# Second layer of a mixture of experts as seven block products in passes two and three, on one core

## The chip, the core and the metric

One core of a Trainium2 chip runs the kernel. Its engines work side by side, each through its own queue in order: TensorE (PE, matmuls; PEld is its weight loads), VectorE (DVE), ScalarE (ACT), GpSimd (POOL) and SyncE (SP, which here issues every DMA). The metric is the time of the program on the device in microseconds, the median of several runs.

## The reference

```python
def _moe_ref(x, w_gate, w1, w2):          # x: attention's output, 2304 tokens x 512
    logits = x @ w_gate                   # 8 experts
    logits = logits - logits.max()
    P = np.exp(logits)
    for _ in range(8):                    # Sinkhorn: rows and columns in turn
        P /= P.sum(1, keepdims=True) + 1e-09
        P /= P.sum(0, keepdims=True) + 1e-09
        P *= N / E
    out = np.zeros((N, D), dtype=np.float32)
    for e in range(E):
        h = np.maximum(x @ w1[e], 0.0)    # 512 -> 1024
        ye = h @ w2[e]                    # 1024 -> 512
        out += P[:, e:e + 1] * ye
    return out
```

`x` comes from a sparse attention (4 batches, 8 heads, 576 positions, head size 64; half of the heads see the last 32 positions, half every 32nd).

## The kernel before

A product of two f32 matrices is made of three matmuls: each operand is split into a part `hi` (ScalarE copies it into the matmul's own f32r format) and the rest `lo` (a subtraction), and hi·hi, hi·lo and lo·hi are summed in PSUM.

The program has three stretches. First the attention, and beside it expert 0 (`layer1`, `layer2`, no gate yet). From about 160 us on, one "slot" after the other of expert 0's second half runs; between its matmuls stand the gate's Sinkhorn iterations (`gating`) and `build_s`, which reads a piece of x back from DRAM (`sx<-xd`), adds and subtracts its blocks and stores the results to DRAM (`sd`). Then come experts 1 to 7, in three passes over 768 tokens each. A pass has 28 groups: 7 experts by 4 slices of the hidden layer, 84 groups in all; `step(g)` is written once for each. In it the order of the code is the order on each engine:

- the last two products of group g-1's first layer (t4 and w22: banks `bb`, `bc`), and DVE's sums and rectified parts of them;
- five products of group g's first layer (`ba`, `bb`, `bc`). The first layer is made of seven block products for eight (blocks of 384 tokens, 256 inputs and 128 hidden units): sums of x blocks (`sd`) with sums of W1 blocks, and sums of the results on DVE (L624). A bank is used for two products with a DVE sum between: t3 adds onto the bank `bb` from which `u2` was read.
- the second layer of group g-1 (`second`, L604): six tiles of 128 tokens, each with 2 hidden slices x 3 matmuls of 128x512; then L611 on DVE multiplies by the gate and adds to `acc`, which holds all 18 token tiles in SBUF.

W1's sums are made in the first pass, split, and stored to DRAM (`wd`, 1792 KB a group); the later passes read them back (L554). W2's blocks are read and split again in every pass (L165 on ACT, L166 on POOL). At a pass's end the seven x operands of the next pass are loaded, each behind the last product that uses the old one (`mul`).

```python
mul(g, "w11", "x11", ba, True)
nc.scalar.activation(m1, ba[:, :TN], AF.Copy)
mul(g, "t2", "s2", bb, True)
plus(u2, bb, m1)
...
mul(g, "t3", "s3", bb, False)
```

## Time and profile before

| | us |
|---|---|
| median of 3 runs | 1611.75 (1611.43 to 1613.36) |
| the profiled execution | 1613.57, span of its core 1611.8 |
| PE busy in the span | 1594.4 (99%) |
| DVE, ACT, POOL busy | 932.4, 493.5, 551.0 |
| DMA | 285.30 MB, mean 177 GB/s |
| mean granted TensorE clock | 0.995 of full speed |

The profiled execution took 1613.57 us, of which 1.8 lie outside the span. "PE busy" is no sign that PE works at its peak, because a matmul's own time overlaps its neighbours'; how fast matmuls follow each other is read from the chain of waits, which gives runs of like instructions with their start and length.

### The profile page before, as it was taken

The page shows a single profiled execution, that of the slowest core. Times are in us where ns is not written, and L with a number is a line of the kernel's source. Part 1 is how long each engine was busy: PE and PEld are TensorE (multiplying, and loading weights), DVE is VectorE, ACT ScalarE, POOL GpSimd, SP SyncE. Part 2 cuts the span into 40 slices and gives each one's busy share as a digit, 9 for nine tenths or more (in the row PEclk, how much of TensorE's full clock was granted, in tenths as well). Part 3 has the DMA queues.
Part 4 walks back from the last instruction along what each step waited for, and adds up shares of the span by engine and source line. Part 5 has one row for each costly group of instructions (what it writes and reads, how often), then busy time and mean ns, then how long its engine had stood idle before and what let it go on. Part 6 is the DMA issues. An engine that isn't in the chain of part 4 may idle for free.

```text
span 1611.8 us, 23077 instructions
## 1 busy us (share of the span) xinstructions
PE 1594.4 (99%) x8779; PEld 1426.0 (88%) x8779; DVE 932.4 (58%) x1896; ACT 493.5 (31%) x1186; POOL 551.0 (34%) x482
## 2 busy tenths in 40 slices
PE   7999999999999999999999999999999999999999
PEld 5888888898989989899898998989989899898997
DVE  4665254466566666666556665566655666556665
ACT  6565222333333333342222222223222222222221
POOL 4222333387677766641312222111111111111111
PEclk8999999999999999999999999999999999999999
DMA  6553424564675656559444544544664344443441
GB/s 202 189 166 111 163 92 170 186 225 167 213 248 170 211 191 212 189 211 342 158 164 164 209 148 157 193 144 163 229 253 165 131 164 143 159 168 131 163 143 73
DMA packets 109455, 285.30 MB, mean 177 GB/s; under 512 B 9120, under 2 KB 62880, under 8 KB 98592
## 3 DMA queue, kind: packets, MB, share of 16 engines
q1 hardware_dynamic: 109344, 283.82, 50.7%
q8 instruction: 69, 1.13, 0.3%
q14 instruction: 42, 0.34, 0.1%
HBM read 208.81 MB, written 74.97 MB: 176 GB/s over the span
## 4 chain that ended last, share of the span: by engine, by line
PE 97%; DVE 1%; DMA 1%; ACT 1%; issue 0%; SPq 0%; POOL 0%; ACTq 0%; POOLq 0%; DVEq 0%
PE yg L604 43%; PE bb L589 16%; PE bc L589 11%; PE ba L589 11%; PE y L414 6%; PE ph L390 6%; PE tp L268 1%; PE pv L281 1%; ACT sm L244 1%; PE sc L225 1%; PE pl L324 1%; PE sc L208 0%; PE pv L295 0%; DMA reg<-sd 0%; DMA qk<-in_qkv 0%; DMA v<-in_qkv 0%
## 5 line engine op out<-in xcount | busy, mean ns | idle before, releaser
L604 PE MATMUL yg<-w2g,h 128*128 128x512 f32 x3024 | 702.8, 390 | 0.0
L604 PEld LDWEIGHTS yg<-w2g,h 128*128 128x128 f32 x3024 | 566.3, 188 | 115.2 <-DVE acc L611 0.4
L611 DVE SCALAR_TENSOR_TENSOR acc<-yg,gate,acc 128x512 f32<-128x512 f32 x504 | 378.2, 751 | 237.8 <-PE yg L604 237.6
L166 POOL TENSOR_TENSOR w2g<-r,w2g 128x512 fp32r<-128x512 f32 x168 | 219.6, 1328 | 721.0 <-ACT w2g L165 721.0
L589 PE MATMUL bb<-reg 128*128 128x384 f32 x1512 | 305.0, 336 | 0.5 <-DVE h L397 0.4
L589 PEld LDWEIGHTS bb<-reg 128*128 128x128 f32 x1512 | 268.0, 188 | 7.7 <-DVE h L397 0.7
L628 ACT ACTIVATE h<-m 128x384 fp32r<-128x384 f32 x84 | 44.2, 526 | 553.6 <-DVE m L624 553.6
L589 PE MATMUL ba<-reg 128*128 128x384 f32 x1008 | 201.7, 334 | 0.0
L589 PE MATMUL bc<-reg 128*128 128x384 f32 x1008 | 201.7, 334 | 0.0
L589 PEld LDWEIGHTS bc<-reg 128*128 128x128 f32 x1008 | 177.8, 188 | 0.0
L589 PEld LDWEIGHTS ba<-reg 128*128 128x128 f32 x1008 | 177.2, 188 | 0.1
L628 ACT ACTIVATE h<-u 128x384 fp32r<-128x384 f32 x168 | 88.3, 526 | 194.2 <-DVE u L624 194.2
L632 DVE SCALAR_TENSOR_TENSOR h<-ba,h 128x384 fp32r<-128x384 f32 x84 | 46.8, 558 | 162.9 <-ACT h L628 162.9
L624 DVE TENSOR_TENSOR u<-bc,u 128x384 f32<-128x384 f32 x168 | 93.7, 557 | 43.4 <-PE bc L589 40.5
L624 DVE TENSOR_TENSOR u<-bb,m 128x384 f32<-128x384 f32 x168 | 93.7, 558 | 37.9 <-PE bb L589 29.5
L390 PE MATMUL ph<-reg,w 128*128 128x256 f32 (+1 forms) x672 | 114.5, 320 | 0.0
L414 PE MATMUL y<-w,h 128*128 128x512 f32 x432 | 110.7, 398 | 0.0
L390 PEld LDWEIGHTS ph<-reg,w 128*128 128x128 f32 x672 | 97.0, 192 | 7.8
L632 DVE SCALAR_TENSOR_TENSOR h<-u,h 128x384 fp32r<-128x384 f32 x168 | 97.7, 582 | 10.1
L628 ACT ACTIVATE h<-ba 128x384 fp32r<-128x384 f32 x84 | 41.3, 492 | 187.8 <-PE ba L589 187.8
L165 ACT ACTIVATE w2g<-r 128x512 fp32r<-128x512 f32 x168 | 95.6, 616 | 0.0
L414 PEld LDWEIGHTS y<-w,h 128*128 128x128 f32 x432 | 78.2, 188 | 17.4
(82 smaller groups left out, 1038.8 us busy)
## 6 DMA issues: line engine op xcount, KB each, us to landing
reg<-wd SPq DMA_DIRECT2D x56, 1792.0 KB, 6.7
wd<-reg SPq DMA_DIRECT2D x28, 1792.0 KB, 6.9
r<-in_w SPq DMA_DIRECT2D x168, 256.0 KB, 2.9
...
```

The costliest lines, as they stand in the source:

```text
L165: nc.scalar.activation(hi, src, AF.Copy)
L166: nc.gpsimd.tensor_tensor(lo, src, hi.bitcast(F32), op=ALU.subtract)
L225: nc.tensor.matmul(scs[j][:m, i, :m], t[sl, i * m : (i + 1) * m], t[sl, nq + i * m : nq + (i + 1) * m], start=True, stop=True,)
L244: nc.scalar.activation(sm[:, i, :], sm[:, i, :], AF.Exp, bias=mx[:rows, i : i + 1], scale=-1.0, accum_out=sums[:rows, j * n + i : j * n + ...
L390: nc.tensor.matmul(ph[:, :n], w[:, i, dt, :], xv(x, dt, c0, n), start=(k == 0), stop=(k == 3 * NDT - 1),)
L414: nc.tensor.matmul(y, h[:, a, i * P : (i + 1) * P], w[:, b, :], start=(ft == 0 and first), stop=(ft == FH - 1 and a == 1),)
L589: nc.tensor.matmul(out[:, :TN], w[:, i, k, :], xops[x][:, xi, k, :], start=(start and n == 0), stop=(n == 5), skip_group_check=True,)
L604: nc.tensor.matmul(y, hg[g, i // 3, f][:, a, o : o + P], w2s[g][f][:, b, :], start=(f == 0 and a + b == 0), stop=(f == 1 and a == 1),)
L611: nc.vector.scalar_tensor_tensor(acc[:, t, :], y, gate[:, t, e : e + 1], acc[:, t, :], op0=ALU.mult, op1=ALU.add)
L624: nc.vector.tensor_tensor(o, bank[:, :TN], s, op=ALU.add)
L628: nc.scalar.activation(hg[g, i, f][:, 0], src[:, :TN], AF.Relu)
L632: nc.vector.scalar_tensor_tensor(h[:, 1], src[:, :TN], 0.0, h[:, 0].bitcast(F32), op0=ALU.max, op1=ALU.subtract)
```

## The change

In the second and third pass, 26 of the 28 groups of a pass (all but the last two, `LAST = 2`) make their second layer from seven block products too. The blocks are 384 tokens, 128 hidden units and 256 outputs. In parts:

- The gate multiplies the rectified first layer (`gated`, on DVE), since products of sums can't be scaled afterwards. The gate is turned into rows beside the first pass (`gate_rows`: 14 small transposes on PE) and read back for all partitions, one expert at a time (`load_gate`).
- POOL adds and subtracts the gated blocks (`s1`, `m1`, `r11`, `s4`) and makes the `lo` parts of all seven operands; ACT makes the `hi` parts.
- `second_strassen`: 7 products x 2 halves of the outputs, 3 matmuls of 128x384 each, outputs transposed (weights stand still, tokens stream). DVE adds each of the 14 results to a sum over the groups (`total`); in the first group of a pass ACT copies it.
- At the end of such a pass `combine` makes four blocks from the seven totals (4 additions on DVE, 3 on POOL, 128x768 each), and `turn` transposes them on PE, 24 transposes of 128x128 a pass, for DVE to add to `acc`.
- The sums of W2's blocks are made in the first pass (`w2_sums`, on DVE and ACT) and stored to DRAM with the split blocks (`w2d`, 2048 KB a group); the later passes read them (1792 KB a group). The `lo` part of W2 moves from POOL to DVE.
- `acc` keeps ten token tiles, expert 0's result of the other tokens goes to DRAM (`yd`), and the sums of x of pass two are made beside expert 0 too, two pieces of `build_s` a slot instead of one; its first additions move from POOL to DVE.

```diff
+    HEAD = 6
+    LATE = range(12, 16)
+    EARLY = [t for t in range(HEAD, NTT) if t not in LATE]
+    acc = big.tile([P, HEAD + len(LATE), D], F32, name="acc")
+    raws = buf.tile([P, 4 * D], F32, name="raws")
+    w2t = buf.tile([P, 8 * D], F32R, name="w2t")
...
                 if u == 0:
-                    nc.scalar.activation(acc[:, t, :], y, AF.Copy)
+                    nc.scalar.activation(o, y, AF.Copy)
                 else:
-                    nc.vector.tensor_tensor(acc[:, t, :], y, acc[:, t, :], op=ALU.add)
+                    nc.vector.tensor_tensor(o, y, o, op=ALU.add)
+                    if t >= HEAD:
+                        nc.sync.dma_start(yd[:, t - HEAD, :], o)
...
         for i in (0, 2):
-            nc.gpsimd.tensor_tensor(
+            nc.vector.tensor_tensor(
                 x[:, i : i + 2], x[:, i : i + 2], s[:, i : i + 2], op=ALU.add
...
+    w2o = [None, w2t.rearrange("p (b n) -> p b n", b=2)]
+    w2sum = acc[:, HEAD : HEAD + 2, :].rearrange("p t d -> p (t d)")
+    Q = 2 * P
+    def w2_sums(g):
+        src, w = w2raw.pop(g), w2o[g % 2]
+        q = src.rearrange("p (n d) -> p n d", d=Q)
+        t = w2sum.rearrange("p (n d) -> p n d", d=Q)
+        nc.vector.tensor_tensor(
+            t[:, 0:2], q[:, 0:1].to_broadcast([P, 2, Q]), q[:, 1:3], op=ALU.subtract
+        )
+        nc.vector.tensor_tensor(t[:, 2], q[:, 2], t[:, 0], op=ALU.subtract)
+        nc.vector.tensor_tensor(t[:, 3], t[:, 2], q[:, 3], op=ALU.subtract)
+        nc.scalar.activation(w[:, 0, 4 * Q :], w2sum, AF.Copy)
+        yield
+        nc.vector.tensor_tensor(
+            w[:, 1, 4 * Q :], w2sum, w[:, 0, 4 * Q :].bitcast(F32), op=ALU.subtract
+        )
+        nc.sync.dma_start(
+            w2d[:, g, :].rearrange("p (b n) -> p b n", b=2), w.bitcast(F32)
+        )
+        yield
     def prep_w2(g):
         if g >= NG:
             return
-        w2s[g] = []
-        for i, src in enumerate(w2raw.pop(g)):
-            t = w2_p.tile([P, 2, D], F32R, tag="w2", name=f"w2g_{g}_{i}")
-            split(t[:, 0], t[:, 1], src)
-            w2s[g].append(t)
-            yield
+        w = w2o[g % 2]
+        if g >= NK:
+            o = Q if strassen(g) else 0
+            n = 8 * Q if strassen(g) else 4 * Q
+            nc.sync.dma_start(
+                w[:, :, o:n].bitcast(F32),
+                w2d[:, g % NK, :].rearrange("p (b n) -> p b n", b=2)[:, :, o:n],
+            )
+            return
+        src = w2raw[g]
+        nc.scalar.activation(w[:, 0, : 4 * Q], src, AF.Copy)
+        yield
+        nc.vector.tensor_tensor(
+            w[:, 1, : 4 * Q], src, w[:, 0, : 4 * Q].bitcast(F32), op=ALU.subtract
+        )
+        yield
+        if g:
+            yield from w2_sums(g)
...
+    def gated(g, o, src, half):
+        p, e, _ = groups[g]
+        nc.vector.scalar_tensor_tensor(
+            o, src[:, :TN], 0.0, gates[p, e][:, half, :], op0=ALU.max, op1=ALU.mult
+        )
+    def form_hi(g, name, src):
+        t = hg[g, name] = form_tile(g, name)
+        nc.scalar.activation(t[:, 0], src, AF.Copy)
+    def form_lo(g, name, src):
+        t = hg[g, name]
+        nc.gpsimd.tensor_tensor(t[:, 1], src, t[:, 0].bitcast(F32), op=ALU.subtract)
...
+    SECOND = (
+        ("a11", 1, 0), ("a22", 7, 3), ("a12", 3, 1), ("s2", 6, 5), ("s3", 5, 6), ("s1", 4, 4),
+        ("s4", 2, 2),
+    )
+    def second_strassen(g):
+        fresh = g % NK == 0
+        w = w2o[g % 2].rearrange("p b (n t d) -> p b n t d", n=8, t=2)
+        for n, (name, wi, ai) in enumerate(SECOND):
+            h = hg.pop((g, name))
+            for d in range(2):
+                y = ps.tile([P, 4 * P], F32, tag="ys"[d], name=f"p_{g}_{n}_{d}")
+                for a, b in ((0, 0), (0, 1), (1, 0)):
+                    nc.tensor.matmul(
+                        y[:, :TN], w[:, b, wi, d, :], h[:, a, :],
+                        start=(a + b == 0), stop=(a == 1),
+                    )
+                o = total[ai][:, d, :]
+                if fresh:
+                    nc.scalar.activation(o, y[:, :TN], AF.Copy)
+                else:
+                    nc.vector.tensor_tensor(o, y[:, :TN], o, op=ALU.add)
...
+    def combine():
+        p1, p2, p3, p4, p5, p6, p7 = total
+        for eng, o, a, b, op in (
+            (nc.gpsimd, p2, p1, p2, ALU.add), (nc.vector, p6, p1, p6, ALU.add),
+            (nc.vector, p7, p6, p7, ALU.add), (nc.vector, p6, p6, p5, ALU.add),
+            (nc.vector, p3, p6, p3, ALU.add), (nc.gpsimd, p4, p7, p4, ALU.subtract),
+            (nc.gpsimd, p5, p7, p5, ALU.add),
+        ):
+            eng.tensor_tensor(o, a, b, op=op)
+    def turn(g, i):
+        y = ps.tile([P, D], F32, tag="ys"[i % 2], name=f"tr_{g}_{i}")
+        o = (i % 3) * P
+        for h, n in enumerate(((2, 1), (4, 3))[i // 3]):
+            for d in range(2):
+                c = (2 * h + d) * P
+                nc.tensor.transpose(y[:, c : c + P], total[n][:, d, o : o + P], ident)
+        nc.vector.tensor_tensor(acc[:, i, :], y, acc[:, i, :], op=ALU.add)
...
+    def finish_first(g, s):
+        m1, u2, u3, bb, bc = part.pop(g)
+        mul(g, "t4", "x22", bb, False)
+        if s:
+            gated(g, u3, u3, 1)
+            form_hi(g, "a22", u3)
+        plus(m1, bb, m1)
+        if s:
+            gated(g, m1, m1, 1)
+        else:
+            relu_hi(g, 1, 0, m1)
+        mul(g, "w22", "s4", bc, False)
+        plus(u2, bc, u2)
+        if not s:
+            relu_hi(g, 0, 1, u2)
+            relu_lo(g, 1, 0, m1)
+            relu_lo(g, 0, 1, u2)
+            return ()
+        gated(g, u2, u2, 0)
+        r11 = r11s.pop(g)
+        s1, s4 = (
+            pools["late"].tile([P, TN], F32, tag=x, name=f"{x}_{g}") for x in ("s1t", "s4t")
+        )
+        nc.gpsimd.tensor_tensor(s1, m1, u3, op=ALU.add)
+        nc.gpsimd.tensor_tensor(m1, m1, r11, op=ALU.subtract)
+        nc.gpsimd.tensor_tensor(r11, s1, r11, op=ALU.subtract)
+        form_lo(g, "a22", u3)
+        nc.gpsimd.tensor_tensor(s4, u2, r11, op=ALU.subtract)
+        return ("a12", u2), ("s2", r11), ("s3", m1), ("s1", s1), ("s4", s4)
...
     def step(g):
 
-        new = g < NG
+        new, G = g < NG, g - 1
+        s = strassen(G)
         w1n, w2n = prep_w1(g + 1), prep_w2(g)
         if new:
             load_w1g(g + 2)
-            load_w2g(g + 1)
+            if g >= NK:
+                next(w2n, None)
+                p, e, j = groups[g]
+                if j == 1:
+                    load_gate(p, e + 1)
+        late = ()
         if g:
-            m1, u2, _, bb, bc = part.pop(g - 1)
-            mul(g - 1, "t4", "x22", bb, False)
-            plus(m1, bb, m1)
-            relu_hi(g - 1, 1, 0, m1)
-            mul(g - 1, "w22", "s4", bc, False)
-            plus(u2, bc, u2)
-            relu_hi(g - 1, 0, 1, u2)
-            relu_lo(g - 1, 1, 0, m1)
-            relu_lo(g - 1, 0, 1, u2)
+            late = finish_first(G, s)
+        if g >= NK:
+            next(w1n, None)
+        if g == 1:
+            for _ in w2_sums(0):
+                pass
+        load_w2g(g + 1)
+        if G >= NK and G % NK == NK - LAST:
+            combine()
...
+        elif s:
+            if new and not strassen(g):
+                relu_lo(g, 1, 1, u3)
+            second_strassen(G)
...
+                if G >= NK and G % NK == NK - LAST:
+                    turn(G, i)
...
+    def sums(*passes):
+        for p in passes:
+            for k in range(2):
+                yield from build_s(p, k)
...
             next(gat, None)
-            next(s0, None)
+            for _ in range(2):
+                next(s0, None)
```

PE, one group's second layer in the second pass; `yg` and `p` are PSUM banks. Before:

```order
L589 MATMUL bb_34_8325<-reg_105 128x384 x6
L604 MATMUL yg_33_0_8367<-w2g_33_0_8267,h00_33_8229 128x512 x3
L604 MATMUL yg_33_0_8367<-w2g_33_1_8278,h01_33_8317 128x512 x3
L604 MATMUL yg_33_1_8376<-w2g_33_0_8267,h00_33_8229 128x512 x3
L604 MATMUL yg_33_1_8376<-w2g_33_1_8278,h01_33_8317 128x512 x3
L604 MATMUL yg_33_2_8384<-w2g_33_0_8267,h00_33_8229 128x512 x3
L604 MATMUL yg_33_2_8384<-w2g_33_1_8278,h01_33_8317 128x512 x3
```

Now:

```order
L651 MATMUL ba_41_9662<-reg_108 128x384 x6
L766 MATMUL p_40_0_0_9719<-a11_40_9557,w2b_3549 128x384 x3
L766 MATMUL p_40_0_1_9724<-a11_40_9557,w2b_3549 128x384 x3
L766 MATMUL p_40_1_0_9729<-a22_40_9639,w2b_3549 128x384 x3
L766 MATMUL p_40_1_1_9734<-a22_40_9639,w2b_3549 128x384 x3
L766 MATMUL p_40_2_0_9739<-a12_40_9672,w2b_3549 128x384 x3
L766 MATMUL p_40_2_1_9744<-a12_40_9672,w2b_3549 128x384 x3
L766 MATMUL p_40_3_0_9749<-s2_40_9675,w2b_3549 128x384 x3
L766 MATMUL p_40_3_1_9754<-s2_40_9675,w2b_3549 128x384 x3
```

The 12 rows of three 128x512 matmuls have become 14 rows of three 128x384, and what was the moving operand (W2) is the one that is loaded.

DVE beside the end of the attention; `h` is expert 0's rectified hidden layer, which PE's next slot waits for, `lt` and `lg` belong to the gate. Before:

```order
L397 SCALAR_TENSOR_TENSOR h_0_1536_2_2427<-ph_0_1536_2_2414,h_0_1536_2_2427 128x256
L328 COPY lt_101<-pl_0_2436 16x512
L397 SCALAR_TENSOR_TENSOR h_0_1536_3_2464<-ph_0_1536_3_2451,h_0_1536_3_2464 128x256
L335 COPY lg_102<-pg_0_2473 128x64
L397 SCALAR_TENSOR_TENSOR h_0_1792_0_2493<-ph_0_1792_0_2480,h_0_1792_0_2493 128x256
L328 COPY lt_101<-pl_512_2504 16x512
```

Now:

```order
L412 SCALAR_TENSOR_TENSOR h_0_1536_2_2417<-ph_0_1536_2_2404,h_0_1536_2_2417 128x256
L343 COPY lt_101<-pl_0_2426 16x512
L501 TENSOR_TENSOR sx_0_0_2436<-sx_0_0_2436 128x2x384
L412 SCALAR_TENSOR_TENSOR h_0_1536_3_2455<-ph_0_1536_3_2442,h_0_1536_3_2455 128x256
L350 COPY lg_102<-pg_0_2464 128x64
L501 TENSOR_TENSOR sx_0_0_2436<-sx_0_0_2436 128x2x384
L412 SCALAR_TENSOR_TENSOR h_0_1792_0_2486<-ph_0_1792_0_2473,h_0_1792_0_2486 128x256
L343 COPY lt_101<-pl_512_2497 16x512
```

The two additions on `sx`, a tile that a DMA fills, stood in POOL's queue and now stand in DVE's, between the `h` of one slot and the next. The pieces come two a slot, so that the first addition follows in the slot that issues the load.

DVE at the end of the second pass, group 54's last sums and group 55's first ones. Before:

```order
L624 TENSOR_TENSOR m1_54_10856<-bb_54_10860,m1_54_10856 128x384
L624 TENSOR_TENSOR u2_54_10857<-bc_54_10861,u2_54_10857 128x384
L632 SCALAR_TENSOR_TENSOR h10_54_10970<-m1_54_10856,h10_54_10970 128x384
L632 SCALAR_TENSOR_TENSOR h01_54_10979<-u2_54_10857,h01_54_10979 128x384
L624 TENSOR_TENSOR u2_55_10984<-bb_55_10987,m1_55_10983 128x384
L632 SCALAR_TENSOR_TENSOR h00_55_11020<-ba_55_10986,h00_55_11020 128x384
```

Now:

```order
L696 TENSOR_TENSOR m1_54_11716<-bb_54_11720,m1_54_11716 128x384
L696 TENSOR_TENSOR u2_54_11717<-bc_54_11721,u2_54_11717 128x384
L708 SCALAR_TENSOR_TENSOR s3_54_11855<-m1_54_11716,s3_54_11855 128x384
L708 SCALAR_TENSOR_TENSOR a12_54_11864<-u2_54_11717,a12_54_11864 128x384
L785 TENSOR_TENSOR total5_7722<-total0_7717,total5_7722 128x768
L785 TENSOR_TENSOR total6_7723<-total5_7722,total6_7723 128x768
L785 TENSOR_TENSOR total5_7722<-total5_7722,total4_7721 128x768
L785 TENSOR_TENSOR total2_7719<-total5_7722,total2_7719 128x768
L696 TENSOR_TENSOR u2_55_11877<-bb_55_11880,m1_55_11876 128x384
```

Between them now stand `combine`'s four additions, and `u2_55`, which PE's product t3 waits for, comes behind them. In step 1 the four instructions of `w2_sums(0)` stand at the same place, ahead of `u2_1`; there they also write `acc` slots whose old content is on its way to DRAM.

## Rows read from the trace of the kernel before

**Rows 1.** The page, its first part: busy time, share of the span, instructions.

```profile
PE 1594.4 (99%) x8779; PEld 1426.0 (88%) x8779; DVE 932.4 (58%) x1896; ACT 493.5 (31%) x1186; POOL 551.0 (34%) x482
```

**Rows 2.** Chain of waits, one group: start us, length us, engine, bank, line, count.

```profile
899.89 1.06 PE bb L589 x6
900.96 1.04 PE bc L589 x6
...
907.20 8.20 PE yg L604 x36
915.40 1.06 PE bb L589 x6
```

**Rows 3.** Windows of 15.5 us: busy us by engine, clock, DMA share, GB/s.

```profile
375.50:391.00 15.50, 15.50 (x80) 14.05 (x79) 9.86 (x16) 5.45 (x12) 10.93 (x11) 1.00 0.56 187
715.50:731.00 15.50, 15.50 (x80) 14.06 (x79) 9.30 (x15) 3.59 (x7) 2.65 (x2) 1.00 0.91 357
731.00:746.50 15.50, 15.50 (x80) 14.05 (x79) 9.30 (x15) 3.59 (x7) 2.64 (x2) 1.00 0.97 388
793.00:808.50 15.50, 15.50 (x80) 14.05 (x79) 9.29 (x16) 3.59 (x7) 4.64 (x4) 1.00 0.44 153
```

**Rows 4.** Groups by line, shapes apart: busy us in all, mean ns of one, idle before.

```profile
L624 DVE TENSOR_TENSOR u<-bb,m 128x384 f32<-128x384 f32 x168 | 93.7, 558 | 37.9 <-PE bb L589 29.5 <-ACT reg L165 7.6
...
L628 ACT ACTIVATE h<-u 128x384 fp32r<-128x384 f32 x168 | 88.3, 526 | 194.2 <-DVE u L624 194.2
...
L423 DVE TENSOR_TENSOR acc<-y,acc 128x512 f32<-128x512 f32 x18 | 11.4, 680 | 2.3 <-PE y L414 2.3
```

**Rows 5.** Chain of waits beside attention and expert 0.

```profile
144.78 0.44 PE tp L268 x4
...
164.94 1.83 PE pl L324 x8
...
169.60 0.35 PE pg L333 x4
...
171.58 1.39 PE y L414 x6
...
247.42 2.39 DVE acc L423 x4
```

**Rows 6.** Line L487 on POOL: ns min/median/max.

```profile
L487 POOL TENSOR_TENSOR sx<-sx x24: 1005/1017/1032, 178.8 to 959.8; 128x384 f32<-128x384 f32 x24
```

**Rows 7.** Line L476 on POOL: ns min/median/max.

```profile
L476 POOL TENSOR_TENSOR sx<-sx x12: 1827/1848/1860, 174.1 to 927.7; 128x768 f32<-128x768 f32 x12
```

**Rows 8.** Timeline around 329 us, DVE and POOL: start us, length us.

```profile
328.49 0.74 POOL L563 TENSOR_TENSOR ru<-ra,rt 128x256 f32<-128x256 f32 x1
328.76 0.88 DVE L632 SCALAR_TENSOR_TENSOR h<-m,h 128x384 fp32r<-128x384 f32 x1
...
329.31 0.94 POOL L564 TENSOR_TENSOR ru<-rb,ru 128x256 f32<-128x256 f32 x1
...
329.57 1.10 DVE L632 SCALAR_TENSOR_TENSOR h<-u,h 128x384 fp32r<-128x384 f32 x1
```

**Rows 9.** Line L632 on DVE: ns min/median/max.

```profile
L632 DVE SCALAR_TENSOR_TENSOR h<-ba,h x84: 556/558/558, 304.0 to 1589.0; 128x384 fp32r<-128x384 f32 x84
```

**Rows 10.** Timeline of POOL, 150 to 260 us.

```profile
174.08 1.84 POOL L476 TENSOR_TENSOR sx<-sx 128x768 f32<-128x768 f32 x1 [17.73 <-DMA sx<-xd]
176.91 1.83 POOL L476 TENSOR_TENSOR sx<-sx 128x768 f32<-128x768 f32 x1 [0.98 <-DMA sx<-xd]
```

**Rows 11.** Timeline of step 1 (its DMA issues and a product).

```profile
312.38 0.95 SPq L146 DMA_DIRECT2D r<-in_w  x2
...
316.48 1.20 PE L589 MATMUL bb<-reg 128*128 128x384 f32 x6
```

**Rows 12.** DMA issues: KB each, median us from issue to landing.

```profile
reg<-wd SPq DMA_DIRECT2D x56, 1792.0 KB, 6.7
...
out<-acc SPq DMA_DIRECT2D x18, 256.0 KB, 3.6
```

More of the change, by code (lines that the diff above doesn't have):

```diff
@@ L155, in load_w @@
         f0 = (fh * FH + ft) * P
[L156 removed]
+        t = raw_slots(1)
         if which == 0:
@@ L593, in product, with strassen, ends, second @@
                 n += 1
-    def second(g, i, tag="y", parts=(0, 1)):
+    LAST = 2
+    def strassen(g):
+        return NK <= g < NG and g % NK < NK - LAST
+    def ends(g):
+        return g % NK == NK - 1
+    def second(g, i, tag=None, parts=(0, 1)):
         p, e, j = groups[g]
         if 0 in parts:
-            yg[g, i] = ps.tile([P, D], F32, tag=tag, name=f"yg_{g}_{i}")
+            yg[g, i] = ps.tile([P, D], F32, tag=tag or "ys"[i % 2], name=f"yg_{g}_{i}")
         y = yg[g, i]
         o = (i % 3) * P
+        w = w2o[g % 2].rearrange("p b (f d) -> p b f d", d=D)
         for f in parts:
@@ L611, in second @@
         nc.vector.scalar_tensor_tensor(
-            acc[:, t, :], y, gate[:, t, e : e + 1], acc[:, t, :], op0=ALU.mult, op1=ALU.add
+            acc[:, i, :], y, gate[:, t, e : e + 1], acc[:, i, :], op0=ALU.mult, op1=ALU.add
         )
-        if e == E - 1 and j == FP - 1:
-            nc.sync.dma_start(out[t * P : (t + 1) * P, :], acc[:, t, :])
+        if ends(g):
+            nc.sync.dma_start(out[t * P : (t + 1) * P, :], acc[:, i, :])
     def mul(g, wn, xn, bank, start):
@@ L619, in mul @@
         product(wops[g % 2][:, :, W_AT[wn]], xn, bank, start)
-        if e == E - 1 and j == FP - 1:
+        if ends(g):
             load_x(p + 1, xn)
@@ new lines, in form_tile @@
+    def form_tile(g, name):
+        return pools["early" if name in ("a11", "a22") else "late"].tile(
+            [P, 2, TN], F32R, tag=name, name=f"{name}_{g}"
+        )
[7 more added lines that the diff above has]
+        nc.scalar.activation(t[:, 0], src, AF.Copy)
@@ L665, in step @@
             nc.scalar.activation(m1, ba[:, :TN], AF.Copy)
+        for name, src in late:
+            form_hi(G, name, src)
+            form_lo(G, name, src)
+        if new:
             mul(g, "t2", "s2", bb, True)
@@ L747, with open_pools, scale @@
         )
-    def sums(p):
-        for k in range(2):
-            yield from build_s(p, k)
-    def scale(t):
-        nc.scalar.activation(acc[:, t, :], acc[:, t, :], AF.Copy, scale=gate[:, t, 0:1])
+    def sums(*passes):
+        for p in passes:
+            for k in range(2):
+                yield from build_s(p, k)
+    def open_pools(side, *names):
+        stacks[side].close()
+        stacks[side] = ExitStack()
+        for name, bufs in names:
+            pools[name] = stacks[side].enter_context(
+                tc.tile_pool(name=name, bufs=bufs, side=side)
+            )
+    def scale(p, i):
+        nc.scalar.activation(
+            acc[:, i, :], acc[:, i, :], AF.Copy, scale=gate[:, 6 * p + i, 0:1]
+        )
     def beside_second_half():
```

162 lines of the change are left out of this document (114 added, 48 removed).

## The prediction

> **What bounds the kernel now.** I read the page's first part, then the chain of waits, then windows, then single lines. The first part puts PE at 1594.4 of 1611.8 us, the next engine, DVE, at 932.4 [rows 1]. Busy time is not pace, so the chain comes next: in the third stretch it never leaves PE. Seven runs of six 128x384 matmuls (1.04 each, the first 1.06) and one run of 36 matmuls of 128x512 (8.20) make a group, and the next starts 15.51 us later (899.89 to 915.40), without a gap [rows 2]. So 128x384 takes 1.04/6 = 0.173 us and 128x512 8.20/36 = 0.228. All 84 groups read alike. A saving on PE therefore comes out in full, as long as nothing else becomes late; everything added elsewhere costs only what it makes PE wait.
>
> **What the change saves.** In 52 groups (26 in each of two passes) 36 x 0.228 = 8.20 becomes 42 x 0.173 = 7.28: 0.92 us a group, 47.8 in all. The group is then 14.59 us long, if the others keep up.
>
> DVE: each of the 14 results comes every 3 x 0.173 = 0.52 us. An addition of 128x384 is busy for 0.558, but like additions that don't need each other overlap by their ends: four of 128x512, 0.680 each, took 2.39, 0.08 less apiece [rows 4, 5]. So one every 0.48, and PE needs no more than the four banks. POOL: four sums and seven `lo` parts of 128x384, 1.02 each [rows 6], are 11.2 of 14.59. Its chain, counted from the group's start: t4 ends at 1.06, DVE adds (0.56) and gates (0.56), so the first sum starts at 2.3; ten operations and one collision with DVE (0.4, below) later the last `lo` part is there at 12.9. PE asks for it at 7.3 (seven products) + 12 x 0.52 + 2 x 0.173 = 13.9. There is 1.0 us left, so I cost the steady groups at nothing; that cover is gone from 1.12 us a POOL operation on. ACT has eight copies of 0.53 [rows 4].
>
> **What it adds on PE.** 48 transposes: four of 128 columns take 0.44 [rows 5], 5.3 us. 14 small ones of the gate at 0.35/4, 1.2. Together 6.5, certain.
>
> **Waits that it makes.** For three of them a fact of the trace matters. DVE instructions with both inputs in SBUF and POOL's take turns: at 328.76 and 329.57 these took 0.88 and 1.10 us, while POOL ran, and POOL's 0.74 became 0.94 [rows 8]. With one input in PSUM the same instruction of the same size never changed (556 to 558 ns in 84) [rows 9]. The 14 additions are of the second kind; the gating of sums, the W2 work and `combine` are of the first.
>
> 1. *End of a pass, twice.* `combine` stands ahead of `u2` of the next group, and PE's t3 adds onto the bank that `u2` reads. 128x768 on DVE is not in the trace: from 558 ns at 384 and 680 at 512 [rows 4], 0.95 ns an element, it is 0.92. DVE comes to it at 3.85 us of the step (two sums, two `lo` parts, each behind ACT). Three additions end at 6.46; POOL's subtraction (1.85 [rows 7]) is ready at 5.7, goes in between, and the fourth runs 8.1 to 9.0. `u2` ends at 9.5, PE wanted t3 at 5.2: 4.35 late. Without turns it is 2.7, with POOL twice in front 5.5. I take 8.7 for two (5.4 to 11).
>
> 2. *`sx` in DVE's queue.* Behind it wait `h` and so expert 0's second layer. Four times the addition waits for a DMA of the same slot. In the first, the pieces land at 174.08 and 176.91, POOL having waited 17.73 for them [rows 10]; DVE would end the first addition at 175.0, then `h`, so PE's `y` at 171.58 [rows 5] starts at 175.35, 3.75 late. The other three come in or near the longer slots (5.5 us), whose slack covers a landing of some 6 us: 1.5 together. 5.2 (3 to 10).
>
> 3. *Step 1.* `w2_sums(0)` writes `acc` slots that must first be stored. The stores stand behind the load issued at 312.38 for 0.95 us [rows 11], and land 3.6 later [rows 12], the first at about 317.2. Then DVE 0.68 + 2 x 0.44, ACT's copy of 1024 (not in the trace; between 0.53, the time of 384, and 1.40, in proportion to it [rows 4]; I take 1.1), DVE 1.17: `u2` at 322, where t3 ran at 316.48 [rows 11]. 5.5 (3 to 8).
>
> 4. *First pass, 27 groups.* DVE, 9.86 of 15.5 us there [rows 3], gets 2 x 1.17 + 0.68 + 2 x 0.44 = 3.9, all with two SBUF inputs, most between the last results of a group; POOL's preparation of W1 (four `lo` parts, three sums, some 7.5 us) lies beside them. If each of the last four waits half a POOL operation, the last result is added 2 to 3 us into the next group. PE minds when `u2` leaves bank `bc` after 4.16, which is when the last result is done after 3.0. So nothing, or 0.65 us a group where every one waits a whole operation; I take 0.25, nearer to nothing, since 3.0 is just reached: 7 (0 to 18). In this sum stand also four `sx` additions and four copies of gate rows in steps without slack.
>
> 5. *DMA at the first change of pass.* The window there moved 388 GB/s at a share of 0.97 [rows 3], so 400 is about all there is. W2's store of groups 26 and 27 (2 x 2.1 MB) and the load for group 28 (1.8) come in front of operands that PE needs, for loads of W2 of 0.5 MB apiece: some 4 MB, 10 us. The two windows had shares of 0.09 and 0.03 free, 1.9 us, and the one behind them a little more: 3 us of cover. 7 (0 to 14). The second change has no stores, and its window has room. In ordinary groups of the first pass 2.1 MB more are 0.35 of a window at that rate, on 0.56: below 1. In later passes 1.8 for 0.5 MB bring 0.44 to about 0.65 [rows 3]; a load lands in 6.7 us [rows 12] and has a group's time. Nothing for both.
>
> **The sum.** 47.8 saved; 6.5 + 8.7 + 5.2 + 5.5 + 7 + 7 = 39.9 given back: 7.9 less than the profiled execution's 1613.57, 1605.7. That execution was 1.8 above the median of the runs, so 1604.
>
> **A rule that speaks against it.** The pace of matmuls is shown by rows for both shapes, 0.173 and 0.228 [rows 2]. The Trainium skill, "TensorE: Matmul & The Clock Gate", section "Back-to-back issue gap", gives for sustained streams about 81 ns at 128 columns and 131 at 512; a straight line between them gives, as an estimate, 114 at 384. By that 42 x 114 = 4.8 us would replace 36 x 131 = 4.7, and the change would save nothing. The rows differ from it for both shapes, and they decide. As a mechanism of this kernel, 42 weight loads for 36 would eat the saving; the 128x384 runs of the first layer reload for every matmul too and keep 0.173.
>
> **Rivals.**
> A. *The waits are mostly hidden.* Terms 4 and 5 nothing, the others at their low ends: 6.5 + 5.4 + 3 + 3 = 17.9 back, 29.9 saved, 1582. For it: DVE has 5.6 us to spare in a group of the first pass, and loads are issued a group ahead of their use. Against: DVE's spare time lies early in the group, its added work late.
> B. *Slower: the first pass.* DVE's last results of each group end later than 3.0 us into the next, because every W2 operation waits for a whole one of POOL. At 0.9 us a group it is 24 for 7: 1621. It decides against the change from 0.67 us a group on (18 us, 1615). For it: rows 8 show both queues waiting in turn. Against: PSUM has four banks for results, and POOL loses W2's `lo` parts.
> C. *POOL is too slow for its chain.* At 1.2 us an operation, 10 x 0.08 in 52 groups is 42: 1646. Against: 1.005 to 1.032 in 24 [rows 6].
> D. *No gain on PE.* 42 weight loads for 36 take what the shorter matmuls save: 39.9 above the median, 1652. The rule of the page named above would make it so.
>
> **How the numbers follow.** No change is within 0.2%, 1608.5 to 1615, about what a measurement can tell. Forecast 0.46, its own range 1596 to 1613 by the ends of terms 1 to 3: 0.31 of it faster, 0.12 same, 0.03 slower. A 0.25, faster. B 0.17: 0.15 slower, 0.02 same. C 0.06 and D 0.02, slower. Anything else 0.04: 0.01, 0.01, 0.02. Faster 0.57, same 0.15, slower 0.28. The range goes from 1577, below A, to 1626, above B; it leaves out C, D and the tails of A and B.
>
> **What would show it.** The second layer in the chain: runs of three 128x384, 7.28 a group, groups 14.59 apart in the last two passes; else C or D. Four gaps on PE: near 172 (3.7 us, behind DVE's `sx`), in step 1 (5.5, behind a store and ACT), in the steps before the ends of passes two and three (4.3, behind DVE at `combine`), and at the start of pass two behind a DMA (7). In the first pass groups of 15.5 to 15.8; at 16.4 B is right, at 15.5 A. The forecast is wrong if steady groups of the later passes are not within 0.1 of 14.59, or if the gaps add to under 15 or over 45 us.

## The result, and the profile after

The changed kernel took 1634.67 us (1632.97 to 1636.3, 4 runs), the kernel before 1612.07 in the same runs: a ratio of 1.0139 (95% interval 1.0122 to 1.0157). It is slower by 1.4%; 1604 was forecast, and 1577 to 1626.

The page's first part (busy us, share of the span, instructions) answers to [rows 1]:

```profile
span 1633.0 us, 25381 instructions
PE 1574.7 (96%) x9153; PEld 1467.9 (90%) x9153; DVE 1238.8 (76%) x2460; ACT 534.1 (33%) x1258; POOL 924.3 (57%) x880
```

PE is busy for 20 us less than before and the span is 21 us longer, so PE now stands idle at some places. It does not in the steady groups. The chain of waits (start, us, what) has there what was forecast, against [rows 2]:

```profile
871.36 7.28 PE p L766 x42
878.64 1.04 PE bb L651 x6
...
885.96 7.28 PE p L766 x42
```

Two second layers start 14.60 us apart, 42 matmuls in 7.28 us. The durations on which the steady groups were costed hold too, DVE's additions of the results and POOL's sums (count, busy us, mean ns, idle before) against [rows 4, 6]:

```profile
L774 DVE TENSOR_TENSOR total<-p,total 128x384 f32<-128x384 f32 x700 | 363.7, 557 | 0.0
...
L821 POOL TENSOR_TENSOR s1t<-m,u 128x384 f32<-128x384 f32 x52 | 52.9, 1016 | 187.5 <-DVE m L741 181.3
```

To find the time, I read in both timelines when each step's t4 (the first `bb` behind a second layer) starts on PE, and subtract from each step what it should take: 15.51 us, 14.59 with a new second layer, 18.15 (15.51 + 6 x 0.44) where the turns are:

| part | before | after | lost | forecast |
|---|---|---|---|---|
| up to step 1 (the front) | 310.21 | 319.12 | 8.9 | 5.2 |
| step 1 | 15.78 | 23.48 | 7.7 | 5.5 |
| steps 2 to 26 (first pass) | 387.66 | 403.04 | 15.4 | 7, and 1.2 for gate rows |
| steps 28 and 29 (first change of pass) | 15.51 and 14.59 due | 24.07, 20.31 | 14.3 | 7 |
| steps 54 and 82 | 14.59 due | 16.23 twice | 3.3 | 0 |
| steps 55 and 83 (`combine`) | 18.15 due | 25.46, 24.36 | 13.5 | 8.7 |
| turns on PE, small rest | | | 5.7 | 5.3 |
| 52 groups | 15.51 | 14.59 | -47.6 | -47.8 |

The sum is +21.2, the difference of the spans. (The front lost more than its row says: the changed kernel's execution was 0.9 us ahead at 160 us, before the sums of x begin.)

Each line below is from a timeline (start, us, engine, line, what, and in brackets how long the engine had stood and behind what). First the stop of step 55, on PE, DVE and POOL:

```profile
1176.09 1.21 PE L651 MATMUL bc<-reg 128*128 128x384 f32 x6
1181.77 2.29 PE L651 MATMUL bb<-reg 128*128 128x384 f32 x6 [4.48 <-DVE u L696]
1183.85 2.12 PE L651 MATMUL ba<-reg 128*128 128x384 f32 x6
```
```profile
1175.84 5.41 DVE L785 TENSOR_TENSOR total<-total,total 128x768 f32<-128x768 f32 x4
1181.17 0.55 DVE L696 TENSOR_TENSOR u<-bb,m 128x384 f32<-128x384 f32 x1
```

The wait is 4.48 us, 4.35 was forecast. But six matmuls then take 2.08 us (1181.77 to 1183.85) instead of 1.04. The windows (busy time and count of PE, PEld, DVE, ACT and POOL, then the granted clock, DMA share, GB/s) show why:

```profile
1171.93:1177.30 5.37, 5.36 (x31) 5.04 (x30) 4.24 (x8) 1.47 (x3) 0.00 (x0) 1.00 0.79 278
...
1181.77:1187.90 6.13, 6.13 (x19) 5.66 (x20) 1.67 (x3) 0.90 (x2) 1.15 (x1) 0.55 1.02 409
1187.90:1197.40 9.50, 9.50 (x56) 7.95 (x54) 7.75 (x12) 0.00 (x0) 0.00 (x0) 1.00 0.30 116
```

Behind the stop PE runs for 6 us at 0.55, nearly all of it at the lower of its two levels (1.2 of 2.4 GHz): 6.13 x 0.45 = 2.8 us more, which no term of the sum had. At the second `combine` the wait is 4.47 us and the clock costs 1.6 (0.74 over the next 6 us). The Trainium skill, "TensorE: Matmul & The Clock Gate", section "Part 1: The HAM clock gate", has it that the throttled state is the default and activity releases it; the rows agree: behind the stop the clock is low and comes back while PE works.

Step 1 and the first change of pass look alike. In step 1 DVE waits for the store of expert 0's results, which lands later than [rows 11, 12] made me think:

```profile
327.59 0.69 DVE L610 TENSOR_TENSOR acc<-raws 128x512 f32<-128x512 f32 x1 [4.46 <-DMA yd<-acc]
```

PE, in step 1 (two lines) and in steps 28 and 29:

```profile
323.30 1.21 PE L651 MATMUL bc<-reg 128*128 128x384 f32 x6
330.72 2.29 PE L651 MATMUL ba<-reg 128*128 128x384 f32 x6 [6.21 <-ACT m L862]
...
765.60 1.28 PE L651 MATMUL ba<-reg 128*128 128x384 f32 x6 [2.18 <-DMA reg<-wd]
...
772.35 2.26 PE L651 MATMUL bb<-reg 128*128 128x384 f32 x6 [3.39 <-DMA reg<-sd]
...
787.07 1.31 PE L651 MATMUL bc<-reg 128*128 128x384 f32 x6 [0.52 <-DMA reg<-sd]
791.31 2.27 PE L651 MATMUL ba<-reg 128*128 128x384 f32 x6 [2.93 <-DMA reg<-wd]
```

At the change PE stands 9.0 us of the 14.3. Behind two of the stops the clock is at its lower level:

```profile
772.35:777.70 5.35, 5.35 (x16) 5.06 (x17) 1.11 (x2) 0.00 (x0) 0.00 (x0) 0.50 0.98 366
791.40:794.70 3.30, 3.30 (x11) 3.30 (x12) 0.00 (x0) 1.02 (x3) 1.78 (x3) 0.50 1.06 434
```

That is (5.35 + 3.30) x 0.50 = 4.3 us more; the last 1.0 is not accounted for. The window 761.1 to 805.5 moved 407 GB/s at a share of 1.01, against 388 at 0.97 in [rows 3]: a full queue, for 44 us.

In the first pass DVE's queue is the late one, and it takes turns with POOL as in [rows 8]. DVE and POOL around the end of a group, in a step that also has an addition of x sums (`sx`):

```profile
504.59 1.40 DVE L683 SCALAR_TENSOR_TENSOR acc<-yg,gate,acc 128x512 f32<-128x512 f32 x2
505.91 2.32 DVE L617 TENSOR_TENSOR w2t<-acc,w2t 128x1024 fp32r<-128x1024 f32 x1
508.16 0.74 DVE L683 SCALAR_TENSOR_TENSOR acc<-yg,gate,acc 128x512 f32<-128x512 f32 x1
508.82 0.94 DVE L501 TENSOR_TENSOR sx<-sx 128x768 f32<-128x768 f32 x1
...
510.15 0.54 DVE L696 TENSOR_TENSOR u<-bc,u 128x384 f32<-128x384 f32 x1
```
```profile
505.86 1.29 POOL L586 TENSOR_TENSOR rt<-rb,ra 128x512 f32<-128x512 f32 x1 [1.93 <-DMA rb<-in_w]
507.23 1.61 POOL L589 TENSOR_TENSOR ru<-ra,rt 128x256 f32<-128x256 f32 x1
```

PE stands 0.85 us at 510.84 behind it. The last result has been added 3.3 us after the step's t4 (505.64); 3.0 was the limit named, and then comes `sx`, ahead of the sums that PE needs.

### The profile page after: what moved, and what is told of

Its sections match the earlier page's. It is cut to its first block, busy times and chain, and to the rows that moved or that the text cites. A ratio compares the mean times of both kernels' runs of the same rounds, so it can differ in the third digit from the quotient of the medians.

```text
span 1633.0 us, 25381 instructions
## 1 busy us (share of the span) xinstructions
PE 1574.7 (96%) x9153; PEld 1467.9 (90%) x9153; DVE 1238.8 (76%) x2460; ACT 534.1 (33%) x1258; POOL 924.3 (57%) x880
## 4 chain that ended last, share of the span: by engine, by line
PE 71%; DVE 16%; ACT 5%; DMA 4%; issue 2%; POOL 1%; SPq 0%; ACTq 0%; POOLq 0%; DVEq 0%
PE p L766 23%; PE bb L651 12%; PE ba L651 8%; PE bc L651 8%; PE yg L676 6%; PE y L429 5%; PE ph L405 5%; DVE acc L683 5%; DMA reg<-wd 2%; DVE acc L614 2%; DVE u L696 1%; ACT reg L180 1%; DMA sx<-xd 1%; DVE acc L613 1%; ACT h L704 1%
## 5 line engine op out<-in xcount | busy, mean ns | idle before, releaser
L774 DVE TENSOR_TENSOR total<-p,total 128x384 f32<-128x384 f32 x700 | 363.7, 557 | 0.0
L651 PEld LDWEIGHTS ba<-reg 128*128 128x128 f32 x1008 | 181.6, 192 | 12.4 <-ACT m L862 6.5
L683 DVE SCALAR_TENSOR_TENSOR acc<-yg,gate,acc 128x512 f32<-128x512 f32 x192 | 138.1, 743 | 12.6 <-PE yg L676 12.5
L429 PE MATMUL y<-w2t,h 128*128 128x512 f32 x432 | 112.3, 401 | 6.5 <-DVE h L412 5.6
L676 PE MATMUL yg<-w2t,h 128*128 128x512 f32 x504 | 117.7, 392 | 0.0
L676 PE MATMUL yg<-w2b,h 128*128 128x512 f32 x504 | 117.1, 390 | 0.0
L766 PE MATMUL p<-s,w2t 128*128 128x384 f32 x624 | 112.3, 334 | 0.0
L766 PE MATMUL p<-s,w2b 128*128 128x384 f32 x624 | 112.3, 334 | 0.0
L766 PEld LDWEIGHTS p<-s,w2t 128*128 128x128 f32 x624 | 108.5, 188 | 0.0
L766 PEld LDWEIGHTS p<-s,w2b 128*128 128x128 f32 x624 | 108.5, 188 | 0.0
L751 POOL TENSOR_TENSOR a<-u,a 128x384 fp32r<-128x384 f32 x104 | 106.0, 1019 | 1.5 <-ACT a L747 1.5
```

Source lines behind the costliest of these rows:

```text
L429: nc.tensor.matmul(y, h[:, a, i * P : (i + 1) * P], w[:, b, :], start=(ft == 0 and first), stop=(ft == FH - 1 and a == 1),)
L651: nc.tensor.matmul(out[:, :TN], w[:, i, k, :], xops[x][:, xi, k, :], start=(start and n == 0), stop=(n == 5), skip_group_check=True,)
L676: nc.tensor.matmul(y, hg[g, i // 3, f][:, a, o : o + P], w[:, b, f, :], start=(f == 0 and a + b == 0), stop=(f == 1 and a == 1),)
L683: nc.vector.scalar_tensor_tensor(acc[:, i, :], y, gate[:, t, e : e + 1], acc[:, i, :], op0=ALU.mult, op1=ALU.add)
L751: nc.gpsimd.tensor_tensor(t[:, 1], src, t[:, 0].bitcast(F32), op=ALU.subtract)
L766: nc.tensor.matmul(y[:, :TN], w[:, b, wi, d, :], h[:, a, :], start=(a + b == 0), stop=(a == 1),)
```

## The experiments

All times are medians; a step's time is from the profile, as in the table. Diffs are against the changed kernel.

**What a stop costs.** `e_busy` lets PE multiply for nothing where it waits anyway (results not used).

```diff
+            if G >= NK and G % NK == NK - LAST:
+                keep(g, 4)          # 4 x 6 matmuls of 128x384 into a free bank
             if g >= NK:
                 mul(g, "t3", "s3", bb, False)
...
+            if g == 1:
+                keep(g, 6)
             mul(g, "w21", "x12", ba, False)
```

> While PE waits, it multiplies for nothing: 24 matmuls of 128x384 (4.2 us, result not used) ahead of t3 in steps 55 and 83, and 36 (6.2 us) ahead of w21 in step 1. The waits themselves stay. Theory (behind a stop of 4.5 to 6.2 us the granted clock is 0.55 to 0.56 for some 4 to 6 us, which costs as much again as 1.6 to 2.7 us): these 2.7, 2.0 and 1.6 us go, steps 55, 83 and 1 take 22.8, 22.4 and 21.9 us instead of 25.46, 24.37 and 23.48, together 5 to 7 us less. Rival (the matmuls behind the stop are slow for another reason, such as transfers at a share of 1.02 or weights read beside DVE and POOL): no change within 1 us.

1628.47 us. Steps 55, 83 and 1 took 22.98, 22.98 and 22.38 us, 5.0 less together. The waits are unchanged: t3 of step 55 starts 9.88 us into its step, 9.84 in the changed kernel. The clock is at its full level behind them (transfers still at a share of 1.03):

```profile
1182.70:1188.20 5.50, 5.50 (x29) 4.88 (x30) 3.37 (x6) 0.90 (x2) 1.17 (x1) 1.00 1.03 409
```

So the slow matmuls follow from the stop, not from the transfers. Of the 1.1 us gained in step 1, 0.8 was lost again in step 2 (17.11 us for 16.28).

**The ends of passes two and three.** `e_end` calls `combine()` behind u3's `relu_lo` and the six `turn`s behind the six results.

> Combine stands behind the new block's u2 and u3 instead of ahead of them, and the six turns behind the six results of the step. Theory (DVE does combine while PE wants t3, and the clock falls in the stop): the stops of 4.48 and 4.47 us and 2 to 2.7 us of slow matmuls behind each go; steps 55 and 83 take about 18.2 us (15.51 + 6 x 0.44) instead of 25.46 and 24.37, 13.4 us less in all. Rival (combine's 5.4 us on DVE now hold up the additions of the results, whose four banks cover only 5.5 us, so that the stop moves behind the fourth result): 4 to 9 us less.

1627.08 us. Steps 55 and 83 took 20.60 and 22.10: 7.1 us less, as the rival had it. The stop at t3 is gone, and a shorter one has come behind the fourth result, where DVE is still in `combine`. The same stop cost different amounts. Behind it the granted clock was 1.00 in step 55, and 0.65 over 4.3 us in step 83; PE in step 55 (two lines) and in step 83:

```profile
1187.30 0.97 PE L676 MATMUL yg<-w2b,s 128*128 128x512 f32 x3 [2.18 <-DVE acc L683]
1188.11 0.85 PE L676 MATMUL yg<-w2b,a 128*128 128x512 f32 x3
...
1604.13 0.97 PE L676 MATMUL yg<-w2b,s 128*128 128x512 f32 x3 [2.18 <-DVE acc L683]
1604.94 1.07 PE L676 MATMUL yg<-w2b,a 128*128 128x512 f32 x3
1605.81 1.48 PE L676 MATMUL yg<-w2b,s 128*128 128x512 f32 x3
```

**The first change of pass.** Later passes load no sums of groups 26 and 27. `e_dead` doesn't make them and stores only the plain half; `e_dma` also issues W2's load behind W1's.

```diff
-        if g:
+        if g >= NK - LAST:
+            w2raw.pop(g)
+            nc.sync.dma_start(w2d[...][:, :, : 4 * Q], w[:, :, : 4 * Q].bitcast(F32))
+        elif g:
             yield from w2_sums(g)
```

> W2 of groups 26 and 27 gets no sums in the first pass and only its plain half is stored (1 MB instead of 2 each): later passes load nothing else of these two groups. Theory (volume: PE's operands at the first change of pass stand in one full queue behind 4 MB of stores): 2.1 MB less at about 400 GB/s are 5.2 us less of stops, and less slow clock behind them: steps 28 and 29 take 37 to 40 us instead of 44.4, and step 27 and 28 lose nothing; the whole 5 to 8 us shorter. Rival (the operands are late because of the order of loads, W2 of group 28 ahead of W1 of group 29, or of the time from PE's last use to landing): under 2 us shorter.

> As the run that left away the sums of groups 26 and 27 and stored only their plain half; and the load of W2 for a group is issued behind that of W1 for the next group, not ahead. Theory (one queue at its full rate, where every byte ahead of a wanted operand counts): 1.8 MB less stand ahead of W1 of group 29, so its wait in step 29 goes; step 29 takes 14.6 to 15.5 us instead of 18.78, step 28 stays at 20; 3 to 4 us less than the run without the sums. Rival (W2 of group 28 then comes late for the second layer, or the bytes are only behind other bytes): steps 28 and 29 together stay at 38 us or more.

1628.66 and 1622.27 us. Steps 28 and 29 together: 44.4, 38.9 (`e_dead`), 34.4 (`e_dma`: 19.67 and 14.69). So the bytes ahead of a wanted operand are what PE waits for: 2.1 MB less gave 5.5 us, the new order 4.5 more, and the stop in step 29 is gone.

**The first pass.** `e_bank` gives ba, bb and bc four banks in turn; `e_lo` moves `lo` of W2's sums, and W2's store, into the next step, behind `plus(u2, bb, m1)`; `e_nopool` leaves out POOL's sums and `lo` parts of W1 from group 2 on.

> The three sums' banks ba, bb, bc take turns on all four banks (two of each tag) instead of bc having one and ba one: t1 of a group then writes where t4 of the group before stood, which DVE has read by m1, one instruction of 0.47 us before u2. Gate rows take a bank of the results. Nothing else moves. Theory (in the first pass t1 waits 0.18 us and loses 0.25 a group because DVE reads bc late): steps 21 to 27 take 15.51 instead of 15.77, those with sums of sx 0.4 to 0.5 less, the whole 7 to 10 us less than the changed kernel. Rival (the late one is ACT's h in ACT's queue, whatever the bank): under 1 us less.

> In the first pass the lo part of W2's sums (1.2 to 1.9 us on DVE between the fourth and sixth result) and the store of W2 move into the next step, behind u2 of t2, where DVE stands 1.72 us idle behind ACT's h. Theory (DVE's queue at the end of a group is what makes u2, and with it bank bc, late): m1 and u2 come over 1 us earlier, steps 21 to 27 take 15.51 instead of 15.77 and those with sx sums 15.5 to 15.8 instead of 16.2 to 16.6; 10 to 14 us less in all. Rival (DVE and POOL taking turns): the moved part now runs beside POOL's two lo parts of W1, takes up to 2.5 us and makes h of ba late; under 4 us less.

> POOL's sums and lo parts of W1 are left out from group 2 on in the first pass (their places keep old values, so the results are not the reference's); ACT copies the raw W1 instead. DVE's work is the same to the instruction. Theory (turns: DVE's instructions with two SBUF inputs wait for POOL's): in the first pass DVE's 128x256 and 128x1024 of the W2 work take 0.42 and 1.2 us throughout instead of 0.85 to 1.4 and 1.25 to 1.9, steps 21 to 27 take 15.51 instead of 15.77 and those with sx sums under 16.1; 8 to 13 us of the first pass's 15.4 go. Rival (DVE has simply too much at the end of a group): steps 21 to 27 stay above 15.65, and under 5 us go.

`e_bank`: 1635.39 us, steps 21 to 26 still 15.74 to 15.78. Bank `bc`, which the prediction named, is not what holds PE: with it free the next product into `ba` waits for m1's copy on ACT, which is queued behind `h` and so behind the same DVE instructions. Its page has PE's weight loads for `ba` (busy us, mean ns, idle us, and behind what):

```profile
L651 PEld LDWEIGHTS ba<-reg 128*128 128x128 f32 x1008 | 178.7, 191 | 20.0 <-ACT m L864 12.8
```

In the changed kernel that row has 12.4 us idle, 6.5 of them behind m.

`e_lo`: 1621.82 us; steps 2 to 26 took 390.4 us instead of 403.0, steps 21 to 26 15.51 each. `e_nopool`: 1616.9 us, 389.7 for the same steps. It shows what made DVE late. The lines view by shape, W2's sums on DVE from 380 to 700 us (busy us, mean ns), of the changed kernel:

```profile
L614 DVE TENSOR_TENSOR acc<-acc,raws 128x256 f32<-128x256 f32 x20 | 28.4, 1418 | 0.7
...
L613 DVE TENSOR_TENSOR acc<-raws,acc 128x256 f32<-128x256 f32 x20 | 16.9, 845 | 0.7
L617 DVE TENSOR_TENSOR w2t<-acc,w2t 128x1024 fp32r<-128x1024 f32 x10 | 14.2, 1416 | 0.0
```

With POOL silent (L622, L623, L626 are L613, L614, L617 there):

```profile
651.15 0.42 DVE L622 TENSOR_TENSOR acc<-raws,acc 128x256 f32<-128x256 f32 x1
651.61 0.43 DVE L623 TENSOR_TENSOR acc<-acc,raws 128x256 f32<-128x256 f32 x1
...
653.27 1.22 DVE L626 TENSOR_TENSOR w2t<-acc,w2t 128x1024 fp32r<-128x1024 f32 x1
```

The same instructions take 1.6 us less a group. So it is the turns, not the amount, that make DVE late; and in `e_lo` the moved `lo` costs PE nothing, because it stands early in the step. The Trainium skill, "SBUF — State Buffer", section "Who interferes with whom", has a DVE instruction with two SBUF inputs contend with a GpSimd instruction that reads SBUF, for a shared port under an exclusive lock. Both traces agree with the contention (1.42 and 0.43 us for the same subtraction); no run here shows the port.

**Step 1.** `e_step1` puts the W2 work of group 0 behind step 1's products; `e_step1b` gives it to POOL there; `e_step0` makes it on POOL in step 0, with scratch in the tile of the x sums.

> The sums of W2 for group 0 are made behind the new block's products instead of ahead of u2 in step 1 (and the load of W2 for group 2, which takes their raw buffer, behind them). Theory (DVE stands at a store of 5.25 us and at ACT's copy while PE wants t3; PE's clock then is at its low level for a few us): the stop of 6.21 us and the 1.6 us of slow matmuls behind it go, step 1 takes 15.8 to 16.5 us instead of 23.48, 7 to 7.7 us less. Rival (the same 4 us of DVE work only move in front of group 0's results, whose four banks then run out): step 1 takes 18 us or more, less than 5.5 us gained.

> In step 1 the sums of W2 for group 0 and their lo part go to POOL, their copy behind the second result on ACT, with scratch of their own in two other slots of acc; DVE does only what every group asks. Theory (DVE's step 1 and 2 are simply too full: 4 us of W2 work for group 0 beside that of group 1, wherever it stands in its queue, as the run that only moved it showed with 19.26 and 19.99 us): steps 1 and 2 take 15.8 to 17 and 16.3 us, 6 to 7.5 us less together than the 39.76 of the changed kernel. Rival (the wait for the store of expert 0's results or POOL's and DVE's turns hold up W1's parts or h instead): steps 1 and 2 together 36 us or more.

> The sums of W2 for group 0 are made in step 0, on POOL, in the free tile of the x sums, with their lo part, and are stored at the end of step 0; nothing else moves. Theory (steps 1 and 2 hold too many instructions of two SBUF inputs, on DVE and POOL together, which take turns; step 0 has room: DVE idle 12 us and POOL 19 us there): steps 1 and 2 take 15.6 to 16 and 16.3 us instead of 23.48 and 16.28, 7 to 8 us less. Rival (it is the store of expert 0's results and the loads behind it that hold up step 1, whatever DVE does): together 36 us or more.

1632.59, 1631.42 and 1628.0 us. Steps 1 and 2 together: 39.76 in the changed kernel, 39.25, 38.15 and 32.80. The first two moved the stop into step 2, where PE stands 2.63 and 4.83 us behind ACT's `h`, which waits for DVE. `e_step0` has no stop in step 1 (15.51), PE's `ba` comes directly behind `bc`; step 2 still loses 1.8:

```profile
325.72 1.20 PE L670 MATMUL bc<-reg 128*128 128x384 f32 x6
326.76 1.20 PE L670 MATMUL ba<-reg 128*128 128x384 f32 x6
```

**The front.** `e_front` adds a `yield` between the loads of `sx` and the additions; `e_pool` puts the additions of passes one and two on POOL; `e_late` goes back to `sums(0)`, one part a slot, on POOL, and makes the sums of passes two and three in the first pass.

> One more yield between the four loads of sx and the first addition, for the sums of passes one and two: the additions stay on DVE, with as much work, but come half a slot or a slot after their loads. Theory (DVE's in-order queue waits for a transfer of the same slot, and h and expert 0's second layer wait behind it): the stops of 3.47 us at 171 us and of 2.13 us at 221 us go, and with them the slow matmuls behind the first; the first step of the groups, 8.9 us later than in the kernel before, is then 1 to 3 us later, and the whole is 6 to 8 us shorter than the changed kernel. Rival (it is the pace of two parts a slot, or the additions' own 0.96 us on DVE, that makes the front longer): less than 2 us shorter.

> The additions of sx for passes one and two, in the front, are back on POOL, as in the kernel before (where only pass one's were made there); those of pass three, in the first pass, stay on DVE. Theory (DVE's in-order queue behind the transfers of sx holds back h): the waits of PE for DVE's h (5.6 us) and the slow matmuls behind them go, the first step starts 1 to 4 us later than before instead of 8.9, the whole is 5 to 8 us less. Rival (twice the sums in the same slots is too much on whichever engine: on POOL, the parts of expert 0's weights wait behind them): the first step still starts 6 us or more late.

> The front makes only the sums of pass one again, one part a slot and with its additions on POOL, as in the kernel before; the sums of passes two and three are both made in the first pass (24 of its 28 steps, additions on DVE). Theory (it is the second set of sums in the front, two parts a slot, and not the engine of its additions): the first step of the groups starts 0 to 2 us later than in the kernel before instead of 8.9; the first pass, where 24 steps instead of 12 now carry parts of sums, loses 0.3 to 0.9 us in four or more of them, 3 to 8 us in all; the whole is 1 to 6 us less. Rival (the front is long for another reason, such as the stores of expert 0's results or the new order of its weight loads): the first step still starts 6 us or more late, and the whole is longer than the changed kernel by the first pass's loss.

1631.14, 1633.21 and 1637.86 us. The first step started at 318.57, 318.93 and 308.67 us (changed kernel 319.12, before 310.21). The wait for DVE's `sx` was only the first in line. In the changed kernel it stops PE for 3.47 us, and the clock is low behind it, with hardly a transfer (the stop, then a window):

```profile
174.59 2.07 PE L429 MATMUL y<-w2t,h 128*128 128x512 f32 x4 [3.47 <-DVE h L412]
```
```profile
174.60:180.00 5.40, 5.40 (x13) 4.23 (x14) 1.36 (x3) 1.19 (x2) 3.93 (x4) 0.50 0.02 5
```

In `e_front` 2.0 us of it stayed and others came; in `e_pool` PE waits for ACT instead, which waits for POOL:

```profile
214.42 5.49 PE L429 MATMUL y<-w2t,h 128*128 128x512 f32 x12 [6.88 <-ACT tail L440]
```

The cause is two parts of sums a slot, whichever engine adds. PE's `y` at 160.47 us in the kernel before and the last one ahead of step 0, at 293.00, are 132.5 us apart, and the same two 142.4 in the changed kernel. In the 13 traces with its slots they are 8.3 to 11.8 us further apart than before, in `e_front` and `e_pool` 9.7 and 10.4, in `e_late` not at all. In the first pass the moved set cost 13 us.

**All together.** `c_all` joined `e_late`, `e_step1b`, `e_dma`, `e_lo`, a `combine` spread over the results, and u3's `lo` behind the second layer in steps 54 and 82: 1606.75 us, where 1586 to 1588 was expected if the waits add up and 1605 to 1612 if not. `c_two` took `e_step0` and the front as it was, and stored W1 of group 27 later: 1602.11 (1590 to 1592 expected if the waits add up, 1598 to 1605 if not); that store then held up the next load of its buffer, and PE for 6.1 us. `c_three` with half of pass two's sums in the front: 1608.21 (1583 to 1587 expected), with two stops where a load and its addition fell into one step. `c_four` mends both; the rest of it is `c_two` without the late store:

```diff
-                gat, s0 = gating(), sums(0, 1)
+                gat, s0 = gating(), sums((0, 0), (0, 1), (1, 0))   # one part a slot, on POOL
...
-    s0 = sums(2)
+    s0 = sums((1, 1), (2, 0), (2, 1))
...
-            next(s0, None)
+            if g > 1:
+                for _ in range((1, 1, 1, 1, 2, 2, 1, 1)[(g - 2) % 8]):
+                    next(s0, None)
```

> Combined, with three of the six sets of x sums in the front, one part a slot, and three in the first pass, where no step has both a load and its addition; W1 of group 27 is stored where it was. Theory (the stops of the combined run before were those of a load and its addition in one step): no step of the first pass above 16.6 us, first pass 3 to 6 us above 15.51 a step, first change 34 to 36 us for two steps; 1590 to 1595. Rival (each set in the first pass costs 4 us or more by POOL's and DVE's turns): 1598 or more.

1590.47 us (1588.56 to 1592.45, 4 runs): 0.9861 of the kernel before (0.9844 to 0.9877), faster than both by 1.4% and 2.7%. `c_five`, all of pass two's sums in the front and the rest the same, took 1591.78 (0.9873, 0.9858 to 0.9887; 1596 to 1599 expected). So as they stand neither place of the sums is clearly better: step 1 starts 4 and 9 us late, the first pass loses 6 and 3. But the 4 us are not the slots'. One part a slot, for pass one's sums and half of pass two's, cost PE nothing there (158.97 to 291.49 us, 132.5 again); they are one stop in step 0, for an operand of x whose load stands behind the sums' last store, and slow matmuls behind it (`c_three` has that stop too, 3.37 us):

```profile
306.12 2.15 PE L676 MATMUL bb<-reg 128*128 128x384 f32 x6 [4.22 <-DMA reg<-sd]
```

No run tried that load earlier. What else is left in `c_four` is 6.2 us at the first change of pass (step 28 21.62, step 29 14.69), 2 at each `combine` and 0.8 each in steps 54 and 82.

## Why the prediction was wrong

- *The saving* was right: 14.59 a group, 47.6 us. Rivals C and D fell. The rule that the Trainium skill, "TensorE: Matmul & The Clock Gate", section "Back-to-back issue gap", gives for sustained streams does not hold here either: 42 matmuls of 128x384 took 7.28 us in the changed kernel too.
- *Term 1, end of a pass* (8.7): 13.5. The mechanism and the wait were right, 4.48 and 4.47 us. The slow clock behind them was left out. Steps 54 and 82 were costed at nothing, without a reason given, and lost 1.64 each: there u3's and ba's `lo` parts on DVE wait for ACT copies queued behind POOL's `s4`, ahead of the first addition to `total` (PE stood 1.37 us at 1166.63). Moving u3's part behind took 0.85 of it.
- *Term 2, `sx`* (5.2): 8.9. The first stop was as forecast (3.47 us), but the cause was too narrow: "Behind it wait `h` and so expert 0's second layer" held for one engine order, and with the additions on POOL the loss was the same. Two parts of sums a slot were too much; at one a slot nothing was lost.
- *Term 3, step 1* (5.5): 7.7. Mechanism right, but the store landed later (DVE starts behind it at 327.59) than estimated (317.2); the wait was 6.2 us, and 1.5 came behind it.
- *Term 4, first pass* (7 of 0 to 18, and 1.2 for gate rows): 15.4. The turns were right, the value was chosen from "since 3.0 is just reached", as if every group stood at the limit alone. The steps with sums of x or gate rows stood past it, most of them 0.3 to 0.9 us a step above the plain ones. That the plain ones lost 0.25, as forecast, is in part luck: bank `bc`, from which the limit was worked out, is not what PE waits for (`e_bank`). The mean, 0.6 us a step, lies between the forecast and rival B's 0.9.
- *Term 5, first change* (7 of 0 to 14): 14.3. The bytes were right (`e_dead`, `e_dma`); nine us of stops for seven, and 5.3 beside them, of which 4.3 are the slow clock.

So every wait that was forecast came, and every one cost more than its term: 68.8 us given back for 39.9. The step that failed is the rule of the sum, "everything added elsewhere costs only what it makes PE wait". About 14 of the 29 us came on top of the waits, in the stretches behind stops: 4.6 at the two `combine`s, 5.3 at the change, 1.5 in step 1, 2.7 in the front (5.4 us at 0.50). By the granted clock 13 of them are the low level; that was tried in three of the five places (`e_busy`) and is read from the clock alone at the change and in the front. The other 15 were sizes: each wait was taken as the only one in its place.

The forecast's own sign could not show this. PE's idle time grew by 41 us (58.3 of the span for 17.4), not "under 15 or over 45 us", and the steady groups were at 14.59. Gaps were counted there, slow matmuls were not.
